# A long causal convolution as a block Toeplitz product, and as a two-step transform with sine matrices

## The chip, the cores and the metric

One core of a Trainium2 chip. The metric is the device time of one execution in microseconds, median of several. The inputs and outputs are float32 (two weights come as float64).

## The reference

Cut to what matters:

```python
B, S, D = 4, 12480, 128
h_filt = (np.maximum(pos_emb @ w1, 0.0) @ w2) * np.exp(-0.01 * np.arange(S))[:, None]
u = x * v
y = irfft(rfft(u, n=2 * S, axis=1) * rfft(h_filt, n=2 * S, axis=0), n=2 * S, axis=1)[:, :S]
h = (x * y).reshape(B * S, D) @ w_in          # 49920 tokens, 128 -> 2048
out = (h * np.cos(h)) @ w_out                 # 2048 -> 128
```

The first part convolves each of 128 channels with a filter as long as the sequence. The second part is a two-layer product over 49,920 tokens.

## The kernel before

It has two stages. In the first, each channel is a block Toeplitz product: the filter lies in DRAM, a DMA lays a shifted copy of it on each partition (a strip), and 98 matmuls for 98 lags accumulate in one PSUM bank.

```python
    def load_strip(pool, d, part):
        ...
        nc.sync.dma_start(
            t[:, 0:w],
            bass.AP(tensor=row.tensor, offset=row.offset, ap=[[1, P], [1, w]]))

    def conv_mm(d, part):
        ...
        for m in range(m0, m1):
            nc.tensor.matmul(
                ps[:, m * B:NC], t[:, (m1 - 1 - m) * P:(m1 - m) * P],
                u[:, 0:NC - m * B], start=(m == 0), stop=(m == NB - 1),
                skip_group_check=True)
```

The second stage takes 512 tokens at a time through 16 chunks of 128 hidden units: an up matmul, the cosine on ScalarE, VectorE and GpSimd, a down matmul.

```python
    def moe_up(pool, n, c):
        ...
        nc.tensor.matmul(ph[:, 0:nt], w_in_sb[:, c * P:(c + 1) * P], ats[n][:, 0:nt],
                         start=True, stop=True)
    ...
    def moe_down(n, c, gt):
        ...
        nc.tensor.matmul(accs[n][:, 0:nt], w_out_sb[:, c, :], gt[:, 0:nt],
                         start=(c == 0), stop=(c == NFC - 1))
```

Of the kernel before, what the change touches and what calls it, by code (L numbers as in the profile page):

```python
# [9 lines left out]
F32 = mybir.dt.float32  # L10
I32 = mybir.dt.int32
# [9 lines left out]
# cos(h) = sin(2 pi f) with f = a - round(a) and a = h / (2 pi) + 1/4.  # L21
INV_TWO_PI = 1.0 / (2.0 * math.pi)
# The float32 just below 2 pi: half a turn stays inside Sin's range of [-pi, pi].
TWO_PI = 6.283185
# Adding it to a float32 and taking it away rounds to the nearest integer.
# [4 lines left out]
def kernel(  # L30
# [11 lines left out]
    """y = x * causal_conv(h_filt, x * v) for each channel, then (g @ w_out) with  # L42
    g = h * cos(h) and h = y @ w_in, all in float32. moe_w_in and moe_w_out come as the
    bits of float64 numbers and are rounded to float32 on the chip.

    The convolution of a channel is a block Toeplitz product over blocks of P positions:
    out block n = sum over lags m of T_m (P x P) times in block n - m. Its moving operand
    has a column for each (block, batch), block outermost, so that a lag is a shift of the
    columns. The filter lies backwards in DRAM, with zeros around it, as hrev[k] =
    h[NB * P - 1 - k]. With row j of a strip at hrev[j:], columns (NB - 1 - m) * P to  # L50
    (NB - m) * P are T_m with its out positions backwards, which the copy of the transposed
    product turns round again.
    """
# [5 lines left out]
    NF = S // P              # full blocks of a sequence  # L59
    TAIL = S - NF * P        # positions in the last, partial block  # L60
    NB = NF + 1              # blocks
    assert D == P and DFF % P == 0 and 0 < TAIL < P and B * P == BANK
    NC = NB * B              # columns of the convolution's moving operand
    NFC = DFF // P
    G = 16                   # channels whose inputs are loaded together
    NG = D // G
    HALF = NB // 2           # lags in the first part of a Toeplitz strip
    PARTS = [(0, HALF), (HALF, NB)]
    SW = max(HALF, NB - HALF) * P
    LAG = 3                  # hidden chunks between an up and its down projection  # L70

    dram = ctx.enter_context(tc.tile_pool(name="dram", bufs=1, space=DRAM))
    hrev = dram.tile([D, NB * P + P - 1], F32, name="hrev")
    ydram = dram.tile([D, NB, B, P], F32, name="ydram")
# [3 lines left out]
    w1_sb = const.tile([FO, FO], F32, name="w1_sb")  # L78
    w2_sb = const.tile([FO, D], F32, name="w2_sb")
    w_in_sb = const.tile([D, DFF], F32, name="w_in_sb")  # L80
    w_out_sb = const.tile([P, NFC, D], F32, name="w_out_sb")
    zeros = const.tile([D, P], F32, name="zeros")
    quarter = const.tile([P, 1], F32, name="quarter")

    ps_acc = ctx.enter_context(tc.tile_pool(name="ps_acc", bufs=2, space=PSUM))
    ps_t = ctx.enter_context(tc.tile_pool(name="ps_t", bufs=2, space=PSUM))
    ps_h = ctx.enter_context(tc.tile_pool(name="ps_h", bufs=4, space=PSUM))
# [5 lines left out]
    def backwards(ap):  # L93
        """`ap` with its last dim, of step 1, turned round."""
        *dims, (step, n) = [list(d) for d in ap.ap]
        assert step == 1
        return bass.AP(tensor=ap.tensor, offset=ap.offset + n - 1, ap=[*dims, [-1, n]])

# [1 line left out]
    conv = ExitStack()  # L100
    upool = conv.enter_context(tc.tile_pool(name="u", bufs=2))
    xvpool = conv.enter_context(tc.tile_pool(name="xv", bufs=2))
    us, xvs = {}, {}

    def load_xv(g, b):
        if b == 0:
            u = upool.tile([P, G, NB, B], F32, name="u")
            nc.gpsimd.memset(u[TAIL:P, :, NF, :], 0.0)  # L108
            us[g] = u
        xv = xvpool.tile([P, 2, NB, G], F32, name="xv")  # L110
        ch = slice(g * G, (g + 1) * G)
        for i, src in enumerate((x, v)):
            nc.sync.dma_start(
                xv[:, i, 0:NF, :],
                src[b, 0:NF * P, ch].rearrange("(n p) d -> p n d", p=P))
            nc.sync.dma_start(xv[0:TAIL, i, NF, :], src[b, NF * P:S, ch])  # L116
        xvs[g, b] = xv

    def mul_xv(g, b):
        xv = xvs.pop((g, b))  # L120
        for rows, n0, n1 in ((P, 0, NF), (TAIL, NF, NB)):
            nc.vector.tensor_tensor(  # L122
                us[g][0:rows, :, n0:n1, b],
                xv[0:rows, 0, n0:n1, :].transpose([0, 2, 1]),
                xv[0:rows, 1, n0:n1, :].transpose([0, 2, 1]),
                op=ALU.mult)

# [1 line left out]
    chunks = [(t0, min(BANK, S - t0)) for t0 in range(0, S, BANK)]  # L129
    pes, wins, peTs = {}, {}, {}  # L130

    def filter_load(pool, i):
        t0, n = chunks[i]
        full, rest = divmod(n, P)
        pe = pool.tile([P, BANK // P, FO], F32, name="pe")
        if full:
            nc.scalar.dma_start(
                pe[:, 0:full, :],
                pos_emb[t0:t0 + full * P, :].rearrange("(m p) c -> p m c", p=P))
        if rest:  # L140
            nc.scalar.dma_start(pe[0:rest, full, :], pos_emb[t0 + full * P:t0 + n, :])
        pos = pool.tile([P, BANK], I32, name="pos")
        nc.gpsimd.iota(pos[:, 0:n], pattern=[[1, n]], base=t0, channel_multiplier=0)
        win = pool.tile([P, BANK], F32, name="win")
        nc.scalar.activation(win[:, 0:n], pos[:, 0:n], AF.Exp, scale=DECAY)
        pes[i], wins[i] = pe, win

    def filter_turn(pool, i):
        n = chunks[i][1]
        pe = pes.pop(i)  # L150
        pt = ps_t.tile([P, BANK], F32, name="pt")
        for m in range(0, n, P):
            r = min(P, n - m)
            transpose(pt[0:FO, m:m + r], pe[0:r, m // P, :])
        peT = pool.tile([FO, BANK], F32, name="peT")
        nc.vector.tensor_copy(out=peT[:, 0:n], in_=pt[0:FO, 0:n])  # L156
        peTs[i] = peT

    def filter_mlp(pool, i):
        t0, n = chunks[i]  # L160
        peT, win = peTs.pop(i), wins.pop(i)
        pa = ps_h.tile([P, BANK], F32, name="ph")
        nc.tensor.matmul(pa[0:FO, 0:n], w1_sb[:, :], peT[:, 0:n], start=True, stop=True)  # L163
        aT = pool.tile([FO, BANK], F32, name="aT")
        nc.scalar.activation(aT[:, 0:n], pa[0:FO, 0:n], AF.Relu)  # L165
        ph = ps_h.tile([P, BANK], F32, name="ph")
        nc.tensor.matmul(ph[:, 0:n], w2_sb[:, :], aT[:, 0:n], start=True, stop=True)  # L167
        hT = pool.tile([D, BANK], F32, name="hT")
        nc.vector.tensor_tensor(backwards(hT[:, 0:n]), ph[:, 0:n], win[:, 0:n], op=ALU.mult)
        nc.gpsimd.dma_start(hrev[:, NB * P - t0 - n:NB * P - t0], hT[:, 0:n])  # L170

# [1 line left out]
    def to_float32(pool, dst, words):  # L173
        raw = pool.tile([P, BANK, 2], U32, name="raw", bufs=2)
        nc.sync.dma_start(raw[:, :, :], words)
        lo, hi = raw[:, :, 0], raw[:, :, 1]
        # 2^exponent with the sign: 0 below float32's normal range, inf above it.
        power = pool.tile([P, BANK], U32, name="power", bufs=2)
# [9 lines left out]
        # The significand: 1 and its first 23 bits, then the other 29 added to it.  # L188
        sig = pool.tile([P, BANK], U32, name="sig", bufs=2)
        rest = pool.tile([P, BANK], U32, name="rest", bufs=2)  # L190
# [4 lines left out]
        nc.vector.tensor_tensor(sig[:, :], sig[:, :], rest[:, :], op=ALU.bitwise_or)  # L195
        nc.vector.tensor_single_scalar(rest[:, :], lo, 0x1FFFFFFF, op=ALU.bitwise_and)
        nc.vector.scalar_tensor_tensor(  # L197
            out=sig[:, :].bitcast(F32), in0=rest[:, :], scalar=2.0 ** -52,
            in1=sig[:, :].bitcast(F32), op0=ALU.mult, op1=ALU.add)
        nc.vector.tensor_tensor(dst, sig[:, :].bitcast(F32), power[:, :].bitcast(F32),  # L200
                                op=ALU.mult)

    in_words = moe_w_in.bitcast(U32).rearrange("d (f w) -> d f w", w=2)
    out_words = moe_w_out.bitcast(U32).rearrange("(c p) (q w) -> p c q w", p=P, w=2)
    weights = []
    for c in range(0, DFF, BANK):
        weights.append((w_in_sb[:, c:c + BANK], in_words[:, c:c + BANK, :]))
# [231 lines left out]
```

## Time and profile before

| | before |
|---|---|
| median time | 8004.58 us (7996.7 to 8016.41, 4 runs) |
| TensorE busy | 99% of the span |
| filter and first loads | to about 220 us |
| Toeplitz convolution | to about 5245 us |
| second part | 2770 us |
| DMA traffic | 995 MB, of which strips 822 MB (256 of 3136 KB, at 1024 bytes) |

A busy TensorE says where the time is spent, not whether it is spent well. The number of matmul columns is what can be attacked. The prediction shows the lines that carry this and how they are read.

### The profile page before, as it was taken

Reading aid. Unit: us, or ns where it says so; the run is one execution under the profiler, and the core shown is the slowest. Engines: PE = TensorE matmul, PEld = TensorE weight load, DVE = VectorE, ACT = ScalarE, POOL = GpSimd, SP = SyncE. Lnnn points to the kernel's source line nnn. Section 1 sums busy time; section 2 is a strip of 40 time slices with the busy share of each in tenths; the row PEclk is TensorE's granted clock in tenths of the full one; section 3 lists DMA queues with packets and bytes.
Section 4 is the critical chain, followed back from the end, with each engine's and each line's share of the span. In section 5 each row is a group of like instructions: output and inputs, shape, how many; then the busy total and the mean of one; then the engine's idle time right before and its main releaser. Section 6 shows DMA issues by size and latency. Waiting matters only on the chain.

```text
span 8012.7 us, 79578 instructions
## 1 busy us (share of the span) xinstructions
PE 7898.3 (99%) x32854; PEld 5406.0 (67%) x32854; DVE 2133.2 (27%) x3656; ACT 2165.6 (27%) x3414; POOL 2014.6 (25%) x1632
## 2 busy tenths in 40 slices
PE   5999999999999999999999999999999999999999
PEld 1788888888888888888888888844444444444444
DVE  4000000000000000000000000056666666666666
ACT  1000000000000000000000000067777777777777
POOL 1000000000000000000000000067777777777776
PEclk9999999999999999999999999999999999999999
DMA  7774774684584685576485444310000011000000
GB/s 99 215 182 170 188 189 169 174 203 166 174 184 183 192 176 184 166 190 180 170 197 178 173 171 166 134 33 28 28 28 28 28 30 30 28 28 28 28 28 20
DMA packets 987802, 994.63 MB, mean 124 GB/s; under 512 B 825680, under 2 KB 927648, under 8 KB 954672
## 3 DMA queue, kind: packets, MB, share of 16 engines
q1 hardware_dynamic: 972128, 979.81, 42.8%
q10 hardware_dynamic: 13344, 3.34, 0.3%
q0 software_dynamic: 1968, 6.39, 0.2%
q8 instruction: 258, 4.23, 0.2%
q14 instruction: 104, 0.85, 0.0%
HBM read 931.76 MB, written 57.74 MB: 123 GB/s over the span
## 4 chain that ended last, share of the span: by engine, by line
PE 98%; DVE 1%; SPq 1%; DMA 0%; ACT 0%; issue 0%; POOL 0%; POOLq 0%; ACTq 0%; DVEq 0%
PE acc L233 62%; PE ph L284 17%; PE acc L308 17%; PE pt L91 2%; SPq L116 1%; PE ph L167 0%; PE ph L163 0%; DMA xv<-in_x_dram 0%; DMA strip<-hrev 0%; ACT aT L165 0%; DVE power L181 0%; DVE u L122 0%; DVE sig L197 0%; DVE sig L195 0%; DVE power L185 0%
## 5 line engine op out<-in xcount | busy, mean ns | idle before, releaser
L233 PE MATMUL acc<-u,strip 128*128 128x392 f32 (+31 forms) x25088 | 4970.2, 361 | 15.0 <-DMA strip<-hrev 15.0
L233 PEld LDWEIGHTS acc<-u,strip 128*128 128x128 f32 x25088 | 4044.8, 198 | 915.2 <-issue 264.4
L293 POOL TENSOR_TENSOR f<-a,k 128x512 f32<-128x512 f32 x1568 | 1983.4, 1265 | 2050.0 <-DMA xb<-in_x_dram 1266.9
L308 PE MATMUL acc<-gt,w_out_sb 128*128 128x512 f32 x3136 | 1596.0, 590 | 2.7 <-DVE gt L301 2.7
L284 PE MATMUL ph<-at,w_in_sb 128*128 128x512 f32 x3136 | 1596.9, 591 | 1.6 <-DVE at L275 1.6
L240 ACT COPY ysb<-acc 128x392 f32<-128x392 f32 x128 | 62.1, 485 | 4959.6 <-PE acc L233 4959.6
L301 DVE TENSOR_TENSOR gt<-ph,cs 128x512 f32<-128x512 f32 x1568 | 1080.3, 689 | 448.1 <-ACT cs L299 444.3
L287 ACT ACTIVATE a<-ph,quarter 128x512 f32<-128x512 f32 x1568 | 1073.9, 685 | 430.2 <-PE ph L284 420.5
L249 DVE COPY yt<-pt 98x512 f32<-98x512 f32 x128 | 88.5, 692 | 3999.7 <-PE pt L91 3999.7
L308 PEld LDWEIGHTS acc<-gt,w_out_sb 128*128 128x128 f32 x3136 | 594.5, 190 | 748.8 <-issue 674.7
L299 ACT ACTIVATE cs<-f 128x512 f32<-128x512 f32 x1568 | 983.6, 627 | 274.8 <-POOL f L293 272.1
L284 PEld LDWEIGHTS ph<-at,w_in_sb 128*128 128x128 f32 x3136 | 581.4, 190 | 655.5 <-issue 652.9
L108 POOL MEMSET u<- 64x64 f32 x8 | 1.2, 146 | 3761.3 <-PE acc L233 3133.1
L290 DVE TENSOR_SCALAR k<-a 128x512 f32<-128x512 f32 x1568 | 679.0, 433 | 454.9 <-ACT a L287 439.0
L122 DVE TENSOR_TENSOR u<-xv 128x1552 f32<-128x1552 f32 x64 | 99.2, 1630 | 845.1 <-DMA xv<-in_v_dram 845.1
L163 PE MATMUL ph<-peT,w_sb 64*64 64x512 f32 (+1 forms) x50 | 48.0, 1063 | 52.6 <-DVE peT L156 52.6
L91 PEld LDWEIGHTS pt<-ident,xb 128*128 128x128 f32 x392 | 49.0, 142 | 55.8 <-issue 32.0
L91 PEld LDWEIGHTS pt<-ident,ot 128*128 128x128 f32 x392 | 49.0, 141 | 51.6 <-issue 50.6
L91 PE MATMUL pt<-ident,ysb 128*98 128x128 f32 x512 | 76.9, 273 | 0.6 <-ACT ysb L240 0.6
L167 PE MATMUL ph<-aT,w_sb 64*128 64x512 f32 (+1 forms) x50 | 50.7, 1117 | 23.4 <-ACT aT L165 23.4
L91 PEld LDWEIGHTS pt<-ident,ysb 128*98 128x98 f32 x512 | 71.0, 169 | 0.8 <-ACT ysb L240 0.7
L275 DVE TENSOR_TENSOR at<-pt,yb 128x512 f32<-128x512 f32 x98 | 66.5, 678 | 5.4 <-DMA yb<-ydram 5.4
(35 smaller groups left out, 441.5 us busy)
## 6 DMA issues: line engine op xcount, KB each, us to landing
strip<-hrev SPq DMA_DIRECT2D x256, 3136.0 KB
ydram<-yt SPq DMA_DIRECT2D x128, 196.0 KB
xv<-in_x_dram SPq DMA_DIRECT2D x32, 776.0 KB
xv<-in_v_dram SPq DMA_DIRECT2D x32, 776.0 KB
xb<-in_x_dram SPq DMA_DIRECT2D x97, 256.0 KB
yb<-ydram SPq DMA_DIRECT2D x97, 256.0 KB
out_dram<-ob SPq DMA_DIRECT2D x97, 256.0 KB
hrev<-hT POOLq DMA_DIRECT2D x24, 256.0 KB, 2.4
```

The lines of the kernel that those rows point to most:

```text
L91: nc.tensor.transpose(dst, src, ident[0:n, 0:n])
L116: nc.sync.dma_start(xv[0:TAIL, i, NF, :], src[b, NF * P:S, ch])
L122: nc.vector.tensor_tensor(us[g][0:rows, :, n0:n1, b], xv[0:rows, 0, n0:n1, :].transpose([0, 2, 1]), xv[0:rows, 1, n0:n1, :].transpose([0, ...
L233: nc.tensor.matmul(ps[:, m * B:NC], t[:, (m1 - 1 - m) * P:(m1 - m) * P], u[:, 0:NC - m * B], start=(m == 0), stop=(m == NB - 1), skip_grou ...
L249: nc.vector.tensor_copy(out=backwards(yt[:, :, :]), in_=pt[0:NB, :].rearrange("n (b i) -> n b i", b=B))
L284: nc.tensor.matmul(ph[:, 0:nt], w_in_sb[:, c * P:(c + 1) * P], ats[n][:, 0:nt], start=True, stop=True)
L287: nc.scalar.activation(a[:, 0:nt], ph[:, 0:nt], AF.Identity, bias=quarter[:, 0:1], scale=INV_TWO_PI)
L290: nc.vector.tensor_scalar(out=k[:, 0:nt], in0=a[:, 0:nt], scalar1=ROUND, scalar2=ROUND, op0=ALU.add, op1=ALU.subtract)
L293: nc.gpsimd.tensor_tensor(f[:, 0:nt], a[:, 0:nt], k[:, 0:nt], op=ALU.subtract)
L299: nc.scalar.activation(cs[:, 0:nt], f[:, 0:nt], AF.Sin, scale=TWO_PI)
L301: nc.vector.tensor_tensor(gt[:, 0:nt], ph[:, 0:nt], cs[:, 0:nt], op=ALU.mult)
L308: nc.tensor.matmul(accs[n][:, 0:nt], w_out_sb[:, c, :], gt[:, 0:nt], start=(c == 0), stop=(c == NFC - 1))
```

## The change

The intent is fewer multiplications. Multiplying two polynomials modulo z^S + i leaves the first S coefficients of the product of real sequences in the real part, so no zero padding to 2S is needed. With S = 104 x 120, that product is taken through a forward transform in two steps (f1 of length 104, f2 of length 120 with a matrix of its own for each of the 104 frequencies k1), a product with the transform of the filter, and two steps back (i1, i2). All are matmuls with matrices of sines that the kernel makes itself: 104 matrices w and 120 matrices T are made once, stored in DRAM and loaded again for each batch. One batch lies in SBUF at a time. In the lines of the profile, u is x times v, w and wd are a matrix w in SBUF and in DRAM, tm and td the same for T, h and hd the transform of the filter, zs and zd the product of x and y that the second part reads. A matmul of these float32 tiles leaves two records in the trace.

The core of the diff, cut (`...` marks cuts):

```diff
-        for m in range(m0, m1):
-            nc.tensor.matmul(
-                ps[:, m * B:NC], t[:, (m1 - 1 - m) * P:(m1 - m) * P],
-                u[:, 0:NC - m * B], start=(m == 0), stop=(m == NB - 1),
-                skip_group_check=True)
...
+    def f1(c):
+        ps = bank()
+        for i in range(2):
+            nc.tensor.matmul(ps[0:N2, i * 2 * N1:(i + 1) * 2 * N1], u[:, :, c + i],
+                             c1[:, :, :].rearrange("p k r -> p (k r)"),
+                             start=True, stop=True)
+        nc.scalar.copy(
+            out=slots[0:N2, 0:2 * N1, c:c + 2].transpose([0, 2, 1]),
+            in_=ps[0:N2, 0:4 * N1].rearrange("p (c j) -> p c j", c=2))
+
+    def f2_mm(k1, i, w, real, imag):
+        ar, ai = slots[0:N2, 2 * k1, :], slots[0:N2, 2 * k1 + 1, :]
+        cols = slice(i * D, (i + 1) * D)
+        nc.tensor.matmul(real[0:N2, cols], w[:, 0, :], ar, start=True, stop=False)
+        nc.tensor.matmul(real[0:N2, cols], w[:, 2, :], ai, start=False, stop=True)
+        nc.tensor.matmul(imag[0:N2, cols], w[:, 1, :], ar, start=True, stop=False)
+        nc.tensor.matmul(imag[0:N2, cols], w[:, 0, :], ai, start=False, stop=True)
...
+        with tc.tile_pool(name="first", bufs=2) as pool:
+            for g in range(G2):
+                load_u(pool, 0, g)
+                if weights:
+                    to_float32(pool, *weights.pop(0))
...
+                for g in range(G1):
+                    real, imag = bank(), bank()
+                    if g + 1 < G1:
+                        h_load(g + 1)
+                    for i in range(G):
+                        k1 = g * G + i
+                        if k1 + 4 < N1:
+                            w_load(k1 + 4)
+                        f2_mm(k1, i, ws.pop(k1), real, imag)
+                    f2_product(pool, g, hs.pop(g), real, imag)
...
+                for c in range(0, D, 2):
+                    i1(c)
+                    if b == 0:
+                        for _ in range(2):
+                            if todo:
+                                n2 = todo.pop(0)
+                                tm = pool.tile([N1, 2, N1], F32, name="tm", bufs=8)
+                                make_matrix(pool, tm[:, :, :], base_t[:, :, :],
+                                            lag_t[:, n2:n2 + 1])
+                                nc.sync.dma_start(td[n2, :, :, :], tm[:, :, :])
+                    if b + 1 < B and c % 4 == 0 and c // 4 < G2:
+                        load_u(pool, b + 1, c // 4)
```

Every DMA of the changed kernel is issued from one queue, SP's, in program order. The second part keeps its matmuls, chunk by chunk.

## The prediction

> **What bounds the kernel now.** I read the page first: busy shares, slices, and the chain that ended last.
>
> ```profile
> PE 7898.3 (99%) x32854; PEld 5406.0 (67%) x32854; DVE 2133.2 (27%) x3656; ACT 2165.6 (27%) x3414; POOL 2014.6 (25%) x1632
> ...
> PE acc L233 62%; PE ph L284 17%; PE acc L308 17%; PE pt L91 2%; SPq L116 1%; PE ph L167 0%; PE ph L163 0%; DMA xv<-in_x_dram 0%; DMA strip<-hrev 0%; ACT aT L165 0%; DVE power L181 0%; DVE u L122 0%; DVE sig L197 0%; DVE sig L195 0%; DVE power L185 0%
> ```
>
> TensorE is never idle: 62% of the chain is the Toeplitz product (line 233), 34% the two matmuls of the second part (lines 284 and 308). Then the stretches (time, busy PE, PEld, DVE, ACT, POOL, granted clock, DMA share, GB/s):
>
> ```profile
> 0.00:200.00 200.00, 115.80 (x189) 30.90 (x189) 83.69 (x135) 29.29 (x49) 28.57 (x54) 1.00 0.79 99
> 2000.00:3000.00 1000.00, 1000.00 (x5199) 825.12 (x5199) 39.74 (x40) 12.61 (x26) 0.29 (x2) 0.95 0.66 182
> 6000.00:7000.00 1000.00, 1000.00 (x2540) 456.43 (x2539) 674.29 (x1200) 749.37 (x1166) 717.17 (x566) 1.00 0.10 28
> ```
>
> Three parts: about 220 us of filter and loading, the Toeplitz convolution to about 5245 us, the second part to the end. The last is PE-bound and its instructions stay the same. The price of a matmul comes from the timeline in the second part and the groups by shape:
>
> ```profile
> 6000.13 1.02 PE L284 MATMUL ph<-at,w_in_sb 128*128 128x512 f32 x2
> 6001.85 1.02 PE L284 MATMUL ph<-at,w_in_sb 128*128 128x512 f32 x2
> ```
> ```profile
> L233 PE MATMUL acc<-u,strip 128*128 128x256 f32 x256 | 76.1, 379 | 0.0
> L233 PE MATMUL acc<-u,strip 128*128 128x128 f32 x256 | 49.2, 274 | 0.0
> L233 PE MATMUL acc<-u,strip 128*128 128x48 f32 x256 | 49.1, 274 | 0.0
> L163 PE MATMUL ph<-peT,w_sb 64*64 64x512 f32 x48 | 47.1, 1084 | 52.6 <-DVE peT L156 52.6
> ```
>
> An up and a down matmul of 512 columns together take 6001.85 - 6000.13 = 1.72 us, so 0.86 us each, 1.68 ns a column. A matmul is two records; from 256 to 128 columns a record loses 105 ns, again 1.64 ns a column for both. Between 128 and 48 columns nothing is saved. So a matmul costs 1.67 ns x max(columns, 128), and 0.213 us at 128. One channel of the convolution, 98 matmuls, takes 39.3 us.
>
> **What the Trainium skill says.** (1) "TensorE: Matmul & The Clock Gate", LDWEIGHTS: a weight load costs its columns over 1.2 GHz, whatever the rows: 107 ns for 128 columns. The trace agrees: a record never goes below the 128-column figure. (2) The same page, Part 1: an idle TensorE falls to half clock. The trace agrees: line 163, with waits between, has records of 1084 ns for 512 columns against 593 in the second part. (3) "SBUF — State Buffer", Door 1, on cachelines: consecutive elements in different 16-byte lines pay a penalty. The multiply of line 122, which reads with a stride of 64 bytes, agrees for VectorE: 3077 ns for 1552 elements, 1.98 ns each, where the slope of contiguous multiplies is (692 - 424) / 256 = 1.05. (4) "DMA: Bandwidth & Descriptors", how many engines: the largest k up to 16 that divides the outer dimension, so 13 engines for a tile of 104 partitions, 15 for 120. No run shows it yet.
>
> ```profile
> L122 DVE TENSOR_TENSOR u<-xv 128x1552 f32<-128x1552 f32 x32 | 98.5, 3077 | 845.1 <-DMA xv<-in_v_dram 845.1
> L301 DVE TENSOR_TENSOR gt<-ph,cs 128x512 f32<-128x512 f32 x1552 | 1073.5, 692 | 444.0 <-ACT cs L299 440.2
> L290 DVE TENSOR_SCALAR k<-a 128x512 f32<-128x512 f32 x1552 | 673.0, 434 | 454.3 <-ACT a L287 438.5 <-POOL f L293 5.3
> 1168.00:1247.00 79.00, 79.00 (x402) 64.53 (x401) 1.38 (x2) 0.97 (x2) 0.00 (x0) 0.93 0.46 171
> hrev<-hT POOLq DMA_DIRECT2D x24, 256.0 KB, 2.4
> ```
>
> The window shows strips alone: 171 GB/s at a share of 0.46, so at most some 370 GB/s on 16 engines. A 256 KB transfer lands 2.4 us after issue: about 1.7 us fixed plus 0.7 us of bytes. I take 2 us fixed. An SP issue in the timeline takes 0.33 to 0.59 us; I take 0.45.
>
> **Removed.** All of line 233: 128 channels x 39.3 us = 5030 us, with the strip loads, the transposes of y and the filter part ahead of it. The span less the second part (98 tiles: 16 x 1.72 + 8 transposes x 0.11 = 28.4 us each, 2770 us in all with the tail) is some 5240 us that goes.
>
> **Added: one forward and one back transform for each batch, and a forward one for the filter.** PE time alone:
> - f1: 128 matmuls x 208 columns x 1.67 = 44 us.
> - f2: 416 matmuls at 128 columns x 0.213 = 89 us.
> - i1: 256 matmuls x 240 columns x 1.67 = 103 us.
> - i2: 240 matmuls x 0.213 = 51 us.
>
> That is 287 us a batch, 1150 for four. But the other engines and the queue now stand in the way, stage by stage:
>
> *f1.* ScalarE evicts 120x416 to columns 512 bytes apart. Contiguous would be 0.50 us (485 ns for 392); with the stride penalty 0.82. So 64 x 0.82 = 52 us, against 44 of PE. **52**. The weights are strided too (200 ns a record if doubled, against 173); the same 52 covers that.
>
> *f2.* For each of 26 groups, PE has 16 matmuls, 3.4 us; VectorE 4 products x 0.69 = 2.8 us; POOL 2 x 1.27. The DMA must bring four w of 173 KB and one h of 492 KB, 1.18 MB. Everything is on the SP queue, in order. In the built order the load of the next h waits for the last product of the group before (two buffers), and the four w of the next group stand behind it. So from the end of group g-1: VectorE 3.0, h issue and bytes 0.45 + 1.4, first w 0.6, fixed 2.0, that is about 7.4 us until group g+1 may start, then 3.4 us to run: 10.8 us for two groups, 5.4 us each. **140 us**, not 89.
>
> *i1.* PE has 1.6 us a pair of channels, ScalarE 0.9 with the penalty, VectorE little. The eight banks are waited for only eight pairs back, and the built waits show none on the slots just written. PE-bound, at the convolution's clock of 0.94: **109 us**. In batch 0, VectorE also makes 120 matrices: two scalar operations of 0.36, one of 156 + 208 x 1.05 = 0.37, gaps 0.1: 1.2 us each, 2.4 a pair, plus 0.35 for the next u. So 60 x 2.75 = **165 us** there.
>
> *i2.* For each of 30 groups PE has 1.7 us; DMA brings four matrices of 87 KB, x of 213 KB, and stores 213 KB. The store waits for the product and the loads of the group after next stand behind it: 1.7 + 0.95 + 2 x 0.45 + 2.0 + 0.5, about 6.1 to 7 us for two groups. 0.77 MB at 13 of 16 engines takes 2.6 us at best. 3.5 us each: **105 us**, not 51.
>
> Batch 0: 52 + 140 + 165 + 105 = 462; others 406; with 5 us at each of 16 changes of stage, 462 + 3 x 406 + 80 = 1760 us.
>
> *Filter and preparation, serial ahead of the batches.* 25 chunks at about 3 us with a half-clock PE, plus the tables: 85. Filter output, 120 matmuls: 30. f1: 52. f2 with matrices made on VectorE: 104 x (2 x 0.40 + 0.53 + 0.1) = 150 (PE 89 hidden). First u with 16 weight conversions: each store waits for the conversion and stands ahead of the next loads: 4.7 us of issue and landing + 0.7 + 4.3 us VectorE = 9.8, x 16 = 157, and 14 further u at 2.3: 190. Sum 507.
>
> **Total:** 507 + 1760 + 2770 + 20 for the reloaded weights and the first z = 5057 us. I predict **5050 us**, 37% less. Working memory in SBUF does not mean little traffic: four batches move 4 x 67 = 270 MB, with the strips' 803 MB gone.
>
> **The rivals.**
> - *PE-bound transforms.* If landing is faster and the queue does not block, f2 falls to 89 and i2 to perhaps 75: 4 x (51 + 30) = 320 us less, 4730. For it: 370 GB/s would be enough for f2's 347. Against it: two h buffers, and the order of the queue.
> - *A cold PE.* Gaps of 1.5 to 2 us in every group may halve the clock, as at the start of the trace. f2 would go to 14 us for two groups, 7 each, and i2 to 4.5: 4 x (42 + 30) = 290 us more, 5340. Against it: the gaps are shorter than those of the filter stage, which reach 28 us.
> - *Strided access worse than doubled.* If ScalarE's writes or the weight loads took four times as long, f1 would be 105 us and i1 115 to 120: 5 x 53 + 3 x 10 = about 295 more. The transposes of y read weights 16 bytes apart and still go at 0.11 us each, which speaks against it for weights.
> - *DMA-bound f2 and i2.* Rows of 1440 and 832 bytes may run well under 370 GB/s; at 180, f2 is 6.6 us a group and i2 4.3: 4 x (31 + 24) = 220 more.
>
> **Range and chances.** The second part, 2770 us, is nearly certain. The 2290 us ahead of it carry an error of some 13%, and the rivals point up a little more than down: 4770 to 5400. Even with every upward rival together, about 5900, the change is faster. Chances: 0.98, 0.01, 0.01.
>
> **What would show it.** Line 233's successors should leave PE about 65% busy in f2 and half busy in i2, with SP waiting on VectorE's products and PE on DMA; i1 should be PE-full; f1 should show PE waiting on ScalarE's copy of 0.8 us; the making of w should show VectorE above 90%; the second part should keep 28.4 us a tile at full clock. Wrong would be: matmul records of twice the length in f2 and i2 (cold clock), PE-full f2, copies above 1.2 us, or a preparation part far from 510 us.

## The result, and the profile after

The changed kernel takes 5285.15 us (median of 4 runs, 5277.3 to 5290.69) against 8004.58 us. The ratio is 0.660 (95% interval 0.659 to 0.661). Such a ratio is the mean time of one kernel's fast runs over that of the other's of the same rounds, so not quite the ratio of the medians. The prediction was 5050 us with a range of 4770 to 5400: the direction and the range held, the point was 235 us low.

The page of the changed kernel, busy shares, slices and the chain by line:

```profile
PE 4583.4 (87%) x16848; PEld 2933.2 (55%) x16848; DVE 2629.9 (50%) x4908; ACT 2746.0 (52%) x4142; POOL 2246.9 (42%) x1787
...
PE   9750776577888798796999999999999999999999
...
PEclk9985877778899798798999999999999999999999
DMA  1353362264644644626000000000000000000000
...
PE ph L393 25%; PE acc L417 25%; PE ps L323 6%; DMA w<-wd 4%; DMA vs<-in_v_dram 4%; DMA tm<-td 3%; PE ps L347 3%; ACT slots L295 3%; PE ps L302 3%; PE ps L303 2%; PE ps L304 2%; PE ps L305 2%; PE pt L95 2%; PE ps L292 1%; DVE phase L228 1%
```

Each slice is 132 us. TensorE is full from the twentieth slice on: the second part, unchanged. Ahead of it, in the slices of the convolution, it has holes, and its granted clock (PEclk) sinks to 0.7 and 0.8 there, to 0.5 in the fourth slice, where TensorE is idle. The chain now names DMA (w, vs, tm) and ScalarE's copy beside TensorE.

Stretches of 25 us from each step, with the columns as in the prediction (length, busy PE, PEld, DVE, ACT, POOL, granted clock, DMA share, GB/s). In order: w made in the filter's f2; the first u; i1 of batch 0; f1; f2; i2; the second part:

```profile
250.00:275.00 25.00, 15.36 (x110) 13.80 (x109) 18.61 (x44) 9.70 (x21) 0.00 (x0) 0.93 0.58 170
425.00:450.00 25.00, 0.00 (x0) 0.00 (x0) 8.74 (x25) 0.00 (x0) 0.00 (x0) 0.50 0.35 98
950.00:975.00 25.00, 13.60 (x39) 10.24 (x39) 13.11 (x39) 9.05 (x18) 0.00 (x0) 0.74 0.26 75
1200.00:1225.00 25.00, 25.00 (x123) 25.00 (x122) 0.00 (x0) 24.97 (x31) 0.00 (x0) 1.00 0.00 1
1300.00:1325.00 25.00, 16.69 (x115) 16.35 (x114) 9.94 (x16) 0.00 (x0) 10.10 (x8) 0.77 0.66 163
1550.00:1575.00 25.00, 19.44 (x111) 17.36 (x111) 4.84 (x7) 0.00 (x0) 0.00 (x0) 0.74 0.71 206
2525.00:2550.00 25.00, 25.00 (x64) 11.26 (x63) 17.41 (x31) 19.17 (x30) 18.67 (x15) 1.00 0.00 1
```

Of these, only f1 and the second part fill TensorE. In the i1 of batch 0, f2, i2 and the making of w no engine is full: that is the sign of a loop of waits. Step by step, from the first matmul of a step's line to the first of the next step (for the first row from the start, for the last to the end; a gap at a change of step is in the row before it; the row of the first u, which has no matmul, begins with its first product):

| step | predicted, us | measured, us |
|---|---|---|
| filter, hidden layer and tables | 85 | 76 |
| filter, output layer | 30 | 52 |
| filter, f1 | 52 | 56 |
| filter, f2 with w made | 150 | 189 |
| first u and weights, TensorE idle | 190 | 181 |
| f1, four batches | 52 each | 56, 54, 54, 54 |
| f2, four batches | 140 each | 174, 171, 172, 174 |
| i1, batch 0 / others | 165 / 109 | 284 / 107, 107, 109 |
| i2, four batches | 105 each | 109, 107, 109, 106 |
| 16 changes of step | 80 | in the rows above |
| weights back, first z | 20 | 10 |
| second part | 2770 | 2776 |
| sum | 5057 | 5287 |

The miss of 230 us is four rows: f2 (+131), i1 of batch 0 (+119), making w (+39) and the filter's output layer (+22), less the 80 set aside for changes of step. The idle time at those changes is in the rows and sums to some 41 us, 24 of it after the i1 of batch 0. The experiments take these rows in turn. All but the last two are single looks (one time, one profile, so their state is unknown). The record names chips 15, 10 and 1 for them and no chip for the changed kernel; its own four runs lie within 14 us.

### The profile page after: what moved, and what is told of

It is laid out like the page before. It is cut to its first block, busy times and chain, and to the rows that moved or that the text cites. A ratio compares the mean times of both kernels' runs of the same rounds, so it can differ in the third digit from the quotient of the medians.

```text
span 5287.4 us, 52816 instructions
## 1 busy us (share of the span) xinstructions
PE 4583.4 (87%) x16848; PEld 2933.2 (55%) x16848; DVE 2629.9 (50%) x4908; ACT 2746.0 (52%) x4142; POOL 2246.9 (42%) x1787
## 4 chain that ended last, share of the span: by engine, by line
PE 71%; DMA 12%; DVE 4%; ACT 4%; issue 1%; SPq 1%; POOL 0%; DVEq 0%; POOLq 0%; ACTq 0%
PE ph L393 25%; PE acc L417 25%; PE ps L323 6%; DMA w<-wd 4%; DMA vs<-in_v_dram 4%; DMA tm<-td 3%; PE ps L347 3%; ACT slots L295 3%; PE ps L302 3%; PE ps L303 2%; PE ps L304 2%; PE ps L305 2%; PE pt L95 2%; PE ps L292 1%; DVE phase L228 1%
## 5 line engine op out<-in xcount | busy, mean ns | idle before, releaser
L316 POOL TENSOR_TENSOR slots<-slots,t 120x512 f32<-120x512 f32 x208 | 262.4, 1266 | 2023.3 <-DVE t L315 2022.7
L326 ACT COPY slots<-ps 104x480 f32<-104x480 f32 x256 | 270.5, 1059 | 810.1 <-PE ps L323 810.1
L323 PE MATMUL ps<-r,slots 120*104 120x240 f32 x2048 | 489.6, 406 | 99.7 <-ACT slots L326 89.1
L295 ACT COPY slots<-ps 120x416 f32<-120x416 f32 x320 | 264.6, 906 | 574.6 <-PE ps L292 574.1
L323 PEld LDWEIGHTS ps<-r,slots 120*104 120x104 f32 x2048 | 444.3, 261 | 144.5 <-ACT slots L326 98.4
L302 PE MATMUL ps<-slots,w 120*120 120x128 f32 x1040 | 255.3, 335 | 249.7 <-DMA w<-wd 181.4
L347 PE MATMUL ps<-slots,tm 104*104 104x128 f32 x1920 | 314.4, 329 | 143.6 <-DMA tm<-td 112.9
L292 PE MATMUL ps<-c,u 104*120 104x208 f32 x1280 | 269.5, 374 | 189.3 <-DVE u L363 188.5
L347 PEld LDWEIGHTS ps<-slots,tm 104*104 104x104 f32 x1920 | 281.8, 211 | 176.6 <-DVE zs L351 68.7
L292 PEld LDWEIGHTS ps<-c,u 104*120 104x120 f32 x1280 | 267.8, 301 | 190.4 <-issue 188.6
```

The source lines that it names most:

```text
L292: nc.tensor.matmul(ps[0:N2, i * 2 * N1:(i + 1) * 2 * N1], u[:, :, c + i], c1[:, :, :].rearrange("p k r -> p (k r)"), start=True, stop=True)
L295: nc.scalar.copy(out=slots[0:N2, 0:2 * N1, c:c + 2].transpose([0, 2, 1]), in_=ps[0:N2, 0:4 * N1].rearrange("p (c j) -> p c j", c=2))
L302: nc.tensor.matmul(real[0:N2, cols], w[:, 0, :], ar, start=True, stop=False)
L323: nc.tensor.matmul(ps[0:N1, i * 2 * N2:(i + 1) * 2 * N2], y[:, :, r], r1[:, r, :, :].rearrange("p c n -> p (c n)"), start=(r == 0), stop=( ...
L347: nc.tensor.matmul(ps[0:N1, i * D:(i + 1) * D], ts[i][:, r, :], slots[0:N1, r * N2 + n2, :], start=(r == 0), stop=(r == 1))
```

## The experiments

### f2: the order of the queue, the clock and the bandwidth

The timeline of f2 in batch 0 of the changed kernel (start, length, engine, line; in brackets the idle time before; selected rows):

```profile
657.08 0.68 DVE L315 TENSOR_TENSOR t<-ps,h 120x512 f32<-120x512 f32 x1
657.79 0.32 SPq L500 DMA_DIRECT2D h<-hd  x1
658.20 1.73 SPq L496 DMA_DIRECT2D w<-wd  x4
661.28 0.32 SPq L500 DMA_DIRECT2D h<-hd  x1
661.69 4.97 SPq L496 DMA_DIRECT2D w<-wd  x4
662.58 0.75 PE L302 MATMUL ps<-slots,w 120*120 120x128 f32 x2 [3.63 <-DMA w<-wd]
663.55 0.63 PE L304 MATMUL ps<-slots,w 120*120 120x128 f32 x2
668.58 0.38 PE L304 MATMUL ps<-slots,w 120*120 120x128 f32 x2
671.51 0.32 SPq L500 DMA_DIRECT2D h<-hd  x1
```

VectorE's last product of a group ends at 657.76; the h load that waits for it is issued at 657.79 and the four w loads behind it at 658.20. TensorE stood idle 3.63 us, until 662.58, for such a w. (The loads at 661.28 and 661.69 are the next group's.) After that gap a pair of records takes 0.63 us, and only six us later 0.38 us: the trace's clock record is at half from 661.6 to 668.5 us and at full after it. Three theories: the queue's order makes the gaps; the half clock makes them longer; or DMA bandwidth sets the pace and both are symptoms.

**e1_h_on_act**: h goes to ScalarE's queue.

```diff
-                    nc.sync.dma_start(hs[g][:, :, :, :], hd[g, :, :, :, :])
+                    nc.scalar.dma_start(hs[g][:, :, :, :], hd[g, :, :, :, :])
```

> Only the loads of h in the forward step f2 of the batches go to ScalarE's queue, so that their wait for VectorE's product no longer stands ahead of the loads of w. Queue theory (the order of the SP queue bounds f2): f2 falls from 173 us a batch to 105 to 125 us, records at half clock vanish, the time falls by about 4 x 55 = 220 us to some 5065 us. Bandwidth theory (1.18 MB a group at the 180 GB/s that the trace shows is all the DMA gives): f2 stays above 165 us and the time within 20 us of 5285.

Measured: 5102.91 us. f2 fell from 171 to 174 us a batch to 120 to 124 us. The window in f2:

```profile
640.00:660.00 20.00, 15.85 (x137) 14.93 (x135) 10.44 (x17) 0.00 (x0) 11.17 (x9) 1.00 0.99 265
```

The granted clock is back at 1.00 and the DMA share is 0.99. So the queue's order was behind both the gaps and the half clock, and freeing it runs into what looks like the next bound, about 260 GB/s of DMA, while TensorE is busy 79%. The total fell by 182 us and f2 by 205: the untouched i2 steps and the i1 of batch 0 were longer in this run than in the changed kernel's profile.

**e2_filler**: the queue as it was, but TensorE is kept from idling with matmuls that nobody reads.

```diff
+                    spare = bank()
+                    for _ in range(6):
+                        nc.tensor.matmul(spare[:, 0:P], ident[:, :], ident[:, :],
+                                         start=True, stop=True)
                     f2_product(pool, g, hs.pop(g), real, imag)
```

> Six unread 128-column matmuls follow each group of f2 in the batches, so that TensorE idles less; nothing else. Clock theory (after each gap the matmuls run at half clock, about 3 us lost in every two groups): f2 falls from 173 us to about 140 us a batch although work was added, the time to some 5155 us, and 128-column records in f2 stay near 273 ns. Queue theory alone (the gaps are the whole loss): f2 stays at 173 us or grows by up to 26 x 1.3 = 33 us, time 5285 to 5420.

Measured: 5204.83 us. f2 fell to 147 to 151 us although 156 matmuls a batch were added.

```profile
680.00:700.00 20.00, 18.12 (x160) 17.80 (x161) 7.45 (x12) 0.00 (x0) 8.84 (x7) 1.00 0.83 204
```

The clock is 1.00 where it was 0.71 to 0.80. So some 25 of the 33 us that f2 lay above the prediction were the half clock, and the queue's chain at full clock is 147 us, near the 140 that was predicted. Of the 52 us a batch that e1 gained, about half was thus the gaps themselves and half the slow matmuls that followed them.

**e9_less_w**: as e1, with two of three matrices of each w loaded (a wrong result).

```diff
-                    nc.sync.dma_start(ws[k1][:, :, :], wd[k1, :, :, :])
+                    nc.sync.dma_start(ws[k1][:, :, :], wd[k1, :, 0:2, :])
...
-        nc.tensor.matmul(real[0:N2, cols], w[:, 2, :], ai, start=False, stop=True)
+        nc.tensor.matmul(real[0:N2, cols], w[:, last, :], ai, start=False, stop=True)
```

> As with h on ScalarE's queue, and in the batches only two of the three matrices of each w are loaded; the third matmul reads the second matrix (a wrong result on purpose: other data, same shapes). Bytes of a group fall from 1.18 to 0.95 MB, the matmuls stay. Bandwidth theory (with the queue freed, f2 is bounded by some 260 GB/s of DMA): f2 falls from 121 us a batch to 97 to 102. Rival (the wait for h and VectorE's products bound what is left): f2 stays above 115.

Measured: 5056.70 us, f2 106 to 109 us.

```profile
660.00:680.00 20.00, 18.76 (x163) 17.95 (x162) 12.41 (x20) 0.00 (x0) 12.51 (x11) 1.00 0.93 239
```

Fewer bytes, less time: bandwidth was the bound after e1, for most of the step at least. Neither 97 to 102 nor "above 115" came; the bandwidth theory is the nearer one. That the fall is smaller than expected fits TensorE, now 94% busy with the DMA share at 0.93, taking over a part of the limit; this was not tested.

### i1 of batch 0: a load behind the stores it waits for

The timeline of the changed kernel in that step (selected rows):

```profile
882.29 0.37 SPq L358 DMA_DIRECT2D u<-in_x_dram  x1
882.75 0.35 SPq L361 DMA_DIRECT2D vs<-in_v_dram  x1
886.16 0.69 DVE L363 TENSOR_TENSOR u<-u,vs 104x512 f32<-104x512 f32 x1 [4.71 <-DMA vs<-in_v_dram]
887.83 0.38 ACT L149 ACTIVATE tm<-phase 104x208 f32<-104x208 f32 x1 [5.06 <-issue]
888.23 3.33 SPq L530 DMA_DIRECT2D td<-tm  x4
891.62 0.37 SPq L358 DMA_DIRECT2D u<-in_x_dram  x1
```

The period is 891.62 - 882.29 = 9.3 us for two pairs of channels. In it VectorE waits 4.7 us for v. Then it makes four matrices, ScalarE takes their sines, SP stores them, and only then is the next u and v loaded. The load of what VectorE needs stands behind the stores of what VectorE makes.

**e3_u_ahead**: same instructions; the product is taken two pairs after its loads were issued.

```diff
-                    if b + 1 < B and c % 4 == 0 and c // 4 < G2:
-                        load_u(pool, b + 1, c // 4)
+                    if b + 1 < B and c % 4 == 0 and c // 4 <= G2:
+                        if c // 4 < G2:
+                            ahead[c // 4] = load_u(pool, b + 1, c // 4)
+                        if c // 4 > 0:
+                            mul_u(*ahead.pop(c // 4 - 1))
```

> In i1 the product u = x * v of a part is taken two pairs of channels after its loads were issued, not at once; same instructions. Chain theory (in batch 0, VectorE waits 4.7 us for each v, whose load stands behind the stores of the matrices that VectorE itself makes): i1 of batch 0 falls from 284 us to 145 to 160 us, bounded by VectorE, and the time to some 5155 us; the other batches stay at 107. Rival (the making of the matrices or their stores bound it): 284 us stays within 20 us.

Measured: 5164.53 us; the i1 of batch 0 went from 284 to 150 us, the others stayed at 108.

```profile
840.00:860.00 20.00, 16.41 (x70) 13.93 (x69) 18.57 (x57) 12.76 (x26) 0.00 (x0) 1.00 0.57 163
```

VectorE is now busy 93%, as the prediction had assumed it was. Without this wait its 165 us would have been near, and a little high.

### Making w: buffers

**e4_six_w**:

```diff
-                    w = pool.tile([N2, 3, N2], F32, name="w", bufs=3)
+                    w = pool.tile([N2, 3, N2], F32, name="w", bufs=6)
```

> The f2 step of the filter, where w is made, has six buffers for w in place of three. Buffer theory (ScalarE waits 62 us for the stores of w to free a buffer): the step falls from 189 us to about 155 us, VectorE above 90% busy, time about 5250 us. Rival (ScalarE's in-order copies of h and the chain of VectorE set it): 180 us or more.

Measured: 5267.55 us. From the first to the last matmul of the step, 181 us became 137.

```profile
220.00:240.00 20.00, 14.84 (x119) 13.47 (x120) 18.95 (x46) 10.99 (x23) 0.00 (x0) 1.00 0.74 219
```

VectorE is busy 95% (74% in the changed kernel's stretch above). The wait for a store to free one of three buffers was the loss. The total fell by only 18 us: in this run the i1 and i2 steps, which the edit does not touch, were some 20 us longer than in the changed kernel's profile. That variation between runs was not looked into.

### The first u, and the store of z in i2

**e5_stores_act**: two stores leave the SP queue.

```diff
-        nc.sync.dma_start(dst, done[:, :])
+        nc.scalar.dma_start(dst, done[:, :])
...
-        nc.sync.dma_start(zd[b, :, g * G:(g + 1) * G, :], zs[:, :, :])
+        nc.scalar.dma_start(zd[b, :, g * G:(g + 1) * G, :], zs[:, :, :])
```

> Two stores leave the SP queue for ScalarE's, in stages that do not touch each other: the converted weights while the first u is loaded, and z in i2. Queue theory for the first u (each store waits for VectorE's conversion and stands ahead of the next loads, as predicted): that stage falls from 181 us to 110 to 125 us. For i2: if the store's place in the queue bounds it, i2 falls from 107 us a batch to 85 to 92; if the DMA does (0.77 MB a group at 210 GB/s, share 0.72), it stays above 100. Time 5285 - 65 = 5220 us with i2 unchanged, 5150 with i2 at 90.

Measured: 5190.90 us. From the last matmul of the step before to the first of the step after, the loading of the first u fell from 189 to 103 us: the order of the queue was nearly half of it; what holds the other 103 us was not looked into. The i2 steps, from first to last matmul, fell from 106 to 109 us to 99 to 103. That is nearer the DMA theory ("above 100") than the queue's (85 to 92): the store's place in the queue cost some 8 us a batch, the rest is not the store's doing. A stretch of i2 in this run:

```profile
1460.00:1480.00 20.00, 16.18 (x85) 14.02 (x84) 3.57 (x6) 0.00 (x0) 0.00 (x0) 0.70 0.74 224
```

The trace most often has 13 packets in flight here, and 15 in e1's f2. Thirteen fifteenths of the 260 GB/s found there is 225 GB/s, by estimate, and 224 is what this stretch moves. That speaks for the DMA as the remaining limit; no run tested it, and the half clock (0.70) is here too.

### f1: two bounds at once

The prediction expected TensorE to wait for ScalarE's strided copy in f1. In the stretch of f1 above, TensorE and ScalarE are both full.

**e6_f1_shared**: every second copy on VectorE.

```diff
-        nc.scalar.copy(
+        copy = nc.scalar.copy if c % 4 == 0 else nc.vector.tensor_copy
+        copy(
```

> Every second eviction of f1 goes to VectorE, nothing else; ScalarE's load in f1 halves. Tie theory (the weight loads of 120 columns 512 bytes apart hold TensorE at 0.84 us a pair, just as long as ScalarE's copy of 0.84 to 0.89): f1 stays at 50 to 54 us. Prediction's reading (ScalarE's strided copy of 0.82 us alone bounds f1): f1 falls to the 44 us of the moving columns, 128 x 208 x 1.67 ns.

**e6_f1_both**: as before, and the weights are read as adjacent columns (a wrong result).

```diff
-            nc.tensor.matmul(..., u[:, :, c + i],
+            nc.tensor.matmul(..., u[:, :, :].rearrange("p n d -> p (n d)")[:, (c + i) * N2:(c + i + 1) * N2],
```

> As the run before, and f1 reads its weights as 120 adjacent columns of u (a wrong result on purpose: other data, same shape). Tie theory: weight loads fall from 300 ns to about 170 to 190 ns a record and f1 to about 45 us, the moving bound. If f1 was already near 45 us in the run before, this changes nothing.

Measured: with the copies shared (5312.97 us) f1 stays at 54 us; with both (5277.22 us) it is 46 to 48 us, batch 0 aside: with these columns its f1 reads u in the order of its loading, and so it starts while u still comes and takes 217 us. The weight loads of the step, first in the run with shared copies, then in the run with both (minimum, median and maximum in ns, then first and last start):

```profile
L292 PEld LDWEIGHTS ps<-c,u x1280: 277/300/324, 128.0 to 2133.5; 104*120 104x120 f32 x183
```
```profile
L292 PEld LDWEIGHTS ps<-c,u x1280: 183/183/325, 127.4 to 2097.6; 104*120 104x120 f32 x183
```

With columns 512 bytes apart a weight load takes 300 ns, adjacent 183. The records start 0.207 us apart in the first case and 0.176 in the second. So the strided weights alone hold the step at 0.83 us a pair, and relieving ScalarE gains nothing. ScalarE's copies follow each other at the same 0.83 us in the changed kernel; whether they would hold the step there by themselves, with adjacent weights and no sharing, was not run.

### The output layer of the filter

**e8_k128**: 128 rows in place of 64, the added ones zero.

```diff
-            rows = bass.AP(tensor=aT.tensor, offset=aT.offset + n2,
-                           ap=[list(aT.ap[0]), [N2, N1]])
+            rows = bass.AP(tensor=aT2.tensor, offset=aT2.offset + n2,
+                           ap=[list(aT2.ap[0]), [N2, N1]])
...
+            nc.vector.memset(w2_sb[FO:P, :], 0.0)
+            nc.vector.memset(aT2[FO:P, 0:S], 0.0)
```

> The output layer of the filter runs with 128 rows in place of 64, the added rows being zeros, so that the whole array is fed; same 120 matmuls. In the changed kernel they take 0.43 us each, half clock, though TensorE never idles there. Activity theory (64 of 128 rows count as half busy and leave the clock low): 0.21 us each after at most 10 us, the stage falls from 52 us to about 30. Stride theory (the weight loads of 104 columns 480 bytes apart take 0.21 us a record): 52 us stays.

Measured: 5308.08 us; the 120 matmuls took 46 us from first to last in place of 51. The changed kernel first, then this run:

```profile
L279 PE MATMUL ps<-w_sb,slots x240: 417/417/554, 75.6 to 126.7; 64*104 64x128 f32 x120
```
```profile
L280 PE MATMUL ps<-w_sb,slots x240: 317/353/557, 73.2 to 119.0; 128*104 128x128 f32 x120
```

The records shorten from 417 to 353 ns (a 128-column record at full clock takes 273), but the step hardly does: the records start 0.213 us apart in the changed kernel and 0.190 in this run. The clock records of the traces tell the theories apart. The changed kernel's trace has none before 133 us, and the view prints 1.00 where there is none. Three runs with the same filter code, e1, e3 and e9, have it, and their records start 0.213 us apart as well. The stretch of this step, first in e1, then in e8:

```profile
70.00:121.00 51.00, 50.81 (x238) 50.81 (x239) 20.06 (x29) 0.14 (x1) 0.00 (x0) 0.50 0.00 1
```
```profile
73.00:119.00 46.00, 45.78 (x240) 45.78 (x240) 20.06 (x29) 0.17 (x1) 0.00 (x0) 0.96 0.00 1
```

With 64 rows the clock stays at half although TensorE is busy all the time. With 128 rows, half of them zeros, it is full from 76.4 us on, 3.2 us after the first of these matmuls; until then these records too start 0.213 us apart, and 0.190 after it. So the activity theory is right about the clock, and wrong about the gain: at full clock something else holds a record at 0.190 us. The weight loads of 104 columns 480 bytes apart (286 ns) are the likely cause, as in f1; adjacent weights were not tried here.

### All together

**b1_queues** joins e1, e3, e4 and e5. **b2_overlap** also removes the idle stage: the first u is loaded while w is made, and the weights are converted, 128 columns at a time, in the i1 steps of batches 1 to 3, through GpSimd's queue. The added lines of b2, cut:

```diff
                     f2_mm(k1, i, w, real, imag)
+                    if k1 % 3 == 0 and k1 // 3 <= G2:
+                        if k1 // 3 < G2:
+                            ahead[k1 // 3] = load_u(pool, 0, k1 // 3)
+                        if k1 // 3 > 0:
+                            mul_u(*ahead.pop(k1 // 3 - 1))
...
-        with tc.tile_pool(name="first", bufs=2) as pool:
...
+                    if b > 0 and c % 10 == 4 and weights:
+                        to_float32(pool, *weights.pop(0))
```

> All the changes of queue and order together: h, z and the converted weights stored or loaded on ScalarE's queue, u taken two pairs after its loads, six buffers for w. If the separate gains (182, 124, 44 and 96 us by stage) add, 5285 - 446 = 4840 us; a shared bound would leave it above 4900.

> As the run before, but the stage that loads the first u with TensorE idle (181 us) is gone: the first u comes while w is made, and the weights are converted in the i1 steps of the later batches, with GpSimd's queue. The making of w should grow from 140 to some 165 us (30 more products of 0.69 us on a full VectorE), the i1 steps stay at 107. Sum: about 4770 us. Rival: the added DMA and VectorE work slows i1 or the making of w by over 60 us, 4830 or more.

Measured, both correct: b1 4784.87 us (ratio to the kernel before 0.597, interval 0.596 to 0.598), b2 4735.45 us (0.591, interval 0.591 to 0.592). The page of b2:

```profile
PE 4434.1 (94%) x16848; PEld 2796.0 (59%) x16848; DVE 2639.1 (56%) x5068; ACT 2740.6 (58%) x4142; POOL 2285.3 (48%) x1851
```

The gains of b1 add: by steps, f2 is shorter by 211 us in all, the i1 of batch 0 by 134, the making of w by 44, the first u by 86 and i2 by 23, together 498 of the 500 us. (The expected 4840 took e1's total for f2, which was too little.) In b2 the making of w takes 191 us from first to last matmul, not 165, so of the 102 us that the idle stage still took in b1 it gives back 54: the net is 49 us in the medians. The kept trace shows where: in that step VectorE waits 37 us for the loads of v, and 30 products of 0.69 us are 21 us more work. It is the wait of i1 again, with v's loads in the queue that the stores of w use; that moving them would end it was not run.

## Why the prediction was right or wrong

**The sum.** That 5240 us of Toeplitz work would go, and that the second part would stay at 2770 us, held: it measured 2776. The range rested on some 2290 us of new work; it measured 2511 with the weights' return. (The strips' "803 MB" are 822, a slip of units that nothing rests on.)

**TensorE's part, right.** A 128-column matmul at 0.213 us and 1.67 ns a column held wherever the clock was full: 62 to 65% of f2's records are at the 128-column figure, and the other batches' i1 took 107 to 109 us against 109 predicted (which assumed a clock of 0.94; it was 0.97 to 0.99).

**f2, the mechanism right, the size off.** "About 7.4 us until group g+1 may start, then 3.4 us to run" came true with a warm TensorE only: 147 us with the filler against 140. The failed step is the weighing of the rival "A cold PE": "the gaps are shorter than those of the filter stage". They were, yet a gap of 3.6 us was enough for six us at half clock. That rival named 7 us a group, or 182 us a batch; 173 was measured. It was right for f2 and should have been in the sum, though not for i2 (4.5 us a group, or 135 us, named; 106 to 109 measured). The prediction's own sign of being wrong, "matmul records of twice the length in f2 and i2", came true in part: about a third of f2's records are longer than the 128-column figure.

**i1 of batch 0, wrong.** "So 60 x 2.75 = 165 us there" added up VectorE's own work and left out its wait. The queue argument that the prediction made for f2 and i2 was not made here, where loads and stores of the same engine's data share the queue. The wait was 134 us; without it the step took 150.

**Making w, off.** "104 x (2 x 0.40 + 0.53 + 0.1) = 150" is near for VectorE (137 us with six buffers) but took three buffers for enough. "VectorE above 90%" came only with six; it was 74%.

**The filter's output layer, off.** "Filter output, 120 matmuls: 30" had neither the half clock (0.213 us a record) nor, behind it, the 0.190 us that remains at full clock. The prediction explained the half clock of the filter in the kernel before by "waits between" (line 163, a 64-row matmul). The runs show that waits are not needed: in e1 the hidden layer (64-row matmuls and transposes) runs at 0.50 from 22 to 69 us with TensorE busy throughout, and from 8 to 22 us, with gaps, it was at full clock. The 1.00 in the prediction's first stretch is no evidence either way: that trace's clock record starts at 226 us.

**f1, right.** 52 predicted, 54 to 56 measured. The copy took 0.89 us against 0.82, and the strided weights 207 ns a record, where the prediction had said "200 ns a record if doubled" and let "the same 52" cover them. Only its sign was wrong: TensorE did not wait for the copy, it was full with the weights. The rival of a fourfold price for stride did not come; that weights 16 bytes apart cost nothing in the transposes of y (0.11 us) did not carry over to 512 bytes.

**i2, the number right, the reason mostly not.** 105 predicted, 106 to 109 measured. The prediction put the time above TensorE's 51 us down to a chain of waits that begins with the store ahead of the loads; taking the store out of the queue (e5) gained 8 us. So the hit is largely luck. What the prediction called "2.6 us at best" for the 0.77 MB of a group would be 3.4 us at the 224 GB/s of e5's i2, by estimate, and 103 us for 30 groups.

**The DMA-bound rival** was right one step later: it is what e1 runs into. The rate was about 260 GB/s, not the 370 that the strips alone had suggested. **PE-bound transforms** was not reached: freeing the queue left f2 at 121 us, not 89.

**Errors that cancelled.** Half of the 80 us for changes of step was not needed, nor 9 us each of the hidden layer and the first u, and hid part of the miss.

## What to carry to other kernels

When a large bound is removed, cost each new stage by its loop of waits, not only by its busiest engine: follow one buffer around (load, compute, free, next load), with everything that stands ahead of it in the same DMA queue. A queue in program order turns a load into a hostage of any store that waits ahead of it; moving one line of code to another queue, or issuing the load two steps earlier, was worth 120 to 180 us here without changing the work. And if a loop leaves TensorE gaps of some microseconds, count its matmuls at half clock until a run shows otherwise; count those of 64 rows so too, even without gaps.

## What the Trainium skill lacked or had wrong

- "TensorE: Matmul & The Clock Gate", LDWEIGHTS, gives the cost by columns alone. The runs show a price for stride: 120 columns 512 bytes apart take 300 ns, adjacent 183 ns, and they pace f1 at 0.207 us a record instead of 0.176.
- "SBUF — State Buffer", on cachelines, has the penalty but no size for ScalarE's writes: copies of 416 and 480 columns to addresses 512 bytes apart took 0.89 and 0.98 us, where the kernel before copied 392 adjacent ones in 0.485 us.
- "TensorE: Matmul & The Clock Gate", Part 1, ties half clock to idle time, and f2 agrees (a gap of 3.63 us, then 0.63 us in place of 0.38 for a pair of records). It lacks what the rows do: with 64 rows the clock stayed at 0.50 for 51 us of busy TensorE (e1, 70 to 121 us), and with 128 rows, half of them zeros, it was full 3.2 us after the first matmul (e8).
- "DMA: Bandwidth & Descriptors", how many engines: counted from the trace, most often 15 packets are in flight at once in e1's f2 (120 partitions) and 13 in i2 (104), which agrees with the largest divisor up to 16 that the page names. The page has no figure for what such transfers reach together: 253 to 267 GB/s at a share of 0.97 to 0.99 in the f2 of e1 and b1.
